# Moving w1's transposes between the gate and the up product, and starting the remaining pages of wo at head 2 of the backward part

## The chip, the cores and the metric

The kernel runs on one core of one Trainium2 chip. The metric is the device time of one execution in microseconds (us). Executions of one kernel spread by about 0.2%, with now and then one that is 0.5% longer, so I compare medians and ratios with 95% intervals, and I read the mechanism in the trace of one profiled execution. The engines are called PE (matrix), DVE (vector), ACT (scalar), POOL (GpSimd) and SP (sync). One megabyte of V, or of an output, is one transfer of one head.

## The reference, cut to what matters

It is one decode step of a transformer layer and its whole gradient: attention over cached K and V of 4 batches x 32 heads x 4096 positions x 128, then a gated feed-forward layer with w1, w3 and w2.

```python
h  = x + attention(layernorm(x), k_cache, v_cache, wq, wo)     # 4 x 1 x 512
h2 = h + (silu(hh @ w1) * (hh @ w3)) @ w2                      # hh = layernorm(h)
# outputs: h2, and by jax.vjp the gradients of x, k_cache, v_cache, wq, wo, w1, w3, w2
```

The gradients of the two caches are 128 heads x 1 MB each. They are outer products: for each head, gv = P (x) dO and gk = dS (x) q. V has to be read twice, once for the forward product and once, transposed, for dP = V dO.

## The kernel before: the parts that the change touches

SBUF has 23 slots of 1 MB. K, V, weights and outputs all take their place in them. Slots are handed out in the order in which they came free, so an output may have to wait until an older output has left its slot.

The middle part lies between forward and backward. It makes the gate and the up product, transposes w1 and w3 in place, and makes dn, from which the first gradients follow:

```python
tunits = deque((nm, i, k) for nm in ("w3", "w1") for i in range(2) for k in range(0, FC, 4))
...
for wi, wt in enumerate((w1, w3)):                 # gate product, then up product (L816 after)
    for fc in range(FC):
        for cc in range(DC):
            nc.tensor.matmul(gu_ps[:, wi, fc, :], lhsT=w13_view(wt, cc)[:, fc * P:(fc + 1) * P], ...)
...                                                # silu and its derivative, on DVE
w13T(len(tunits), "ssssvsvssvvsvsvv")              # 112 transposes; "s"/"v": copied back by ACT/DVE
for jj in range(DC):
    for (lt, wt) in ((d_upT_bf, w3), (d_gateT_bf, w1)):
        ...                                        # dn, 112 products
while len(free) > 2:
    load_V2()
```

For dP a head needs its column of dO, and for gv it needs its row of dO. Both come from wo, in four pages of eight heads (eight of the model's 32, so 32 of the 128 that are counted as head 0, 1, 2 and so on below). Page 0 is done in the middle part. The others are done piece by piece by a generator that is stepped once per head. For each page it has four wo units (eight transposes and one copy) and then one step that makes the columns and rows of dO:

```python
def dO_columns(h0, h1, ps, tag):
    ...                                                    # PE: 32 products into dOT_ps
    nc.vector.tensor_copy(out=dOT_bf[:, s0:s1], in_=dOT_ps[:, s0:s1])              # L735
    nc.vector.tensor_tensor(out=dOT_f[:, s0:s1], in0=dOT_bf..., in1=OT_f..., op=ALU.mult)  # L736
def dO_rows(h0, h1, ps_, tag_):
    nc.tensor.transpose(pq[0:s1, :], dOT_bf[:, 0:s1], ident_b[:])                  # L741
    ...
    nc.tensor.matmul(c_ps[:, s0:s1], lhsT=ones_f[:], rhs=dOT_f[:, s0:s1], ...)     # L744
    nc.vector.tensor_copy(out=c_rep[:, s0:s1], in_=c_ps[:, s0:s1])                 # L745

def rest_of_dO():
    for pg in range(1, H // 8):
        while wo_units and wo_units[0] < 4 * (pg + 1):
            woT_unit(psT, wo_units.popleft(), "s")
            yield
        dO_columns(8 * pg, 8 * pg + 8, psg, "gps")
        dO_rows(8 * pg, 8 * pg + 8, psg, "gps")
        mid_w["wo"][pg].give()                             # the page's slot comes free here
        yield
```

The backward part:

```python
S0 = 15
...
front(0)
step("o")                       # one step of rest_of_dO
for s in range(NH):
    prefetch()
    if s + 1 < NH:
        ...
        front(s + 1)            # PE, ACT: every 4th head replicate rows; 32 transposes of V; dP
        grad_V(s + 1)           # DVE: gv (2.29 us), then its 1 MB output
    grad_K(s)                   # DVE: dS, gk (2.29 us), then its 1 MB output
    if s < S0:
        step("o")
    else:
        step("s", ...)          # side work: gradients of the weights
```

## Time and profile before

| before | |
|---|---|
| time | 1732.32 us (1732.11 to 1735.81, 3 runs); with a fourth run, 1735.24, the median is 1733.78 |
| profiled execution | 1741.45 us, span of the core 1739.7 us |
| moved by DMA | 707.86 MB, at 419 GB/s in a good stretch |
| underfed stretch at the turn from forward to backward | 702 to 748 us, 12.6 us lost |
| first gv given to DMA | 712.7 us |
| dO of page 1 | at head 3, 743 to 745 us |

To read the profile, "lost" is the time that a stretch would have saved at 419 GB/s: its length times (1 - GB/s / 419). Lost isn't the same as idle. In the windows that the prediction shows, the column before GB/s is the share of time in which the DMA engines were busy; it is about 1.01 in a full window.

### The profile page before, as it was taken

The numbers are of one execution on the slowest core, as the hardware profiler recorded it, in microseconds if no ns is written. First come the engines' busy times: TensorE is split into PE (matmuls) and PEld (weight loads), VectorE is DVE, ScalarE is ACT, GpSimd is POOL, SyncE is SP. The second block draws the span as 40 slices with busy tenths as digits, with TensorE's granted clock in tenths as the row PEclk, the third lists the DMA queues.
The fourth block names the chain that finished last, engine by engine and source line by source line (L and its number), as shares of the span: only waits on it lengthen the run. The fifth ranks groups of instructions, "written<-read, shape, count | busy, mean of one in ns | idle before, by whom it ended". The sixth has DMA issues, their size and how long they took to land.

```text
span 1739.7 us, 44047 instructions
## 1 busy us (share of the span) xinstructions
PE 1331.1 (77%) x19014; PEld 1123.0 (65%) x19014; DVE 1253.8 (72%) x1388; ACT 958.4 (55%) x1469; POOL 445.6 (26%) x808
## 2 busy tenths in 40 slices
PE   5888888888888888877888887856685878778662
PEld 4667666676666666766777777755563556556562
DVE  5989899889998996567567667665583555665673
ACT  3455445444444454666555564546674667667552
POOL 1211232222222221223123222222231232223331
PEclk8999999999999999676555565558665655555555
DMA  9999999999999999899999999999999999999997
GB/s 398 410 419 418 419 418 419 419 416 418 411 419 408 418 404 392 317 397 418 416 415 421 419 412 414 413 417 419 423 411 368 420 416 406 412 405 410 411 418 290
DMA packets 107179, 707.86 MB, mean 407 GB/s; under 512 B 11284, under 2 KB 18976, under 8 KB 24040
## 3 DMA queue, kind: packets, MB, share of 16 engines
q1 hardware_dynamic: 66880, 422.60, 59.3%
q0 software_dynamic: 39712, 282.37, 39.8%
q8 instruction: 149, 2.44, 0.5%
q14 instruction: 46, 0.38, 0.1%
q10 hardware_dynamic: 392, 0.07, 0.0%
HBM read 422.59 MB, written 282.34 MB: 405 GB/s over the span
## 4 chain that ended last, share of the span: by engine, by line
DMA 42%; DVE 6%; PE 6%; ACT 5%; issue 4%; POOL 0%; SPq 0%; POOLq 0%; DVEq 0%; ACTq 0%
DMA out_dram<-gk 27%; DMA out_dram<-gv 6%; ACT VT L760 4%; DMA wq<-in_A_wq_dram 3%; DVE gk L1114 2%; PE pt_tps L759 2%; DVE gv L1114 2%; DMA out_dram<-gw 2%; DMA out_dram<-gwo 2%; DMA w<-in_B_w_dram 1%; DMA wo<-in_A_wo_dram 1%; PE gps L907 1%; PE dP_ps L1108 0%; DVE PK L418 0%; PE pt_w L562 0%
## 5 line engine op out<-in xcount | busy, mean ns | idle before, releaser
L760 ACT COPY VT<-pt_tps 128x1024 bf16<-128x1024 bf16 x512 | 492.7, 1015 | 244.6 <-PE pt_tps L759 131.3
L759 PE MATMUL pt_tps<-ident_b,V 128*128 128x128 bf16 x4096 | 456.8, 294 | 118.9 <-ACT VT L760 97.7
L759 PEld LDWEIGHTS <-V 128*128 128x128 bf16 x4096 | 405.5, 139 | 184.6 <-issue 154.9
L1114 DVE TENSOR_TENSOR gv<-P,reps 128x4096 bf16<-128x4096 bf16 x128 | 293.5, 2293 | 258.3 <-DMA out_dram<-gk 98.0
L1114 DVE TENSOR_TENSOR gk<-dS,reps 128x4096 bf16<-128x4096 bf16 x128 | 293.4, 2292 | 81.8 <-DMA out_dram<-gv 48.2
L433 PE MATMUL M_ps<-PK,Vn 128*128 128x130 bf16 x4096 | 285.6, 222 | 51.0 <-DMA Vn<-in_A_v_cache_dram 50.4
L418 DVE TENSOR_TENSOR PK<-Kn,PK 128x4096 bf16<-128x4096 bf16 x128 | 292.3, 2284 | 33.5 <-POOL PK L414 33.2
L433 PEld LDWEIGHTS <-Vn 128*128 128x128 bf16 x4096 | 252.4, 99 | 72.6 <-DMA Vn<-in_A_v_cache_dram 66.9
L325 DVE STREAM_TRANSPOSE KT<-Kn 128x512 f32<-128x512 f32 (+1 forms) x321 | 250.7, 797 | 0.3 <-issue 0.2
L320 ACT COPY KT<-pt_tps 128x1024 bf16<-128x1024 bf16 x128 | 129.5, 1012 | 191.0 <-PE pt_tps L319 149.5
L1108 PE MATMUL dP_ps<-dOT_bf,VT 128*128 128x1 bf16 x4096 | 152.6, 166 | 67.8 <-ACT VT L760 64.5
L1108 PEld LDWEIGHTS <-VT 128*128 128x128 bf16 x4096 | 141.1, 104 | 80.3 <-ACT VT L760 76.8
L1139 POOL DMA_DIRECT2D out_dram<-gk x128 | 68.4, 534 | 360.9 <-DVE gk L1114 225.2
L1125 POOL DMA_DIRECT2D out_dram<-gv x128 | 68.7, 537 | 325.2 <-DVE dSt L1132 258.1
L331 POOL TENSOR_TENSOR W<-qrep,wmask 128x128 bf16<-128x128 bf16 x128 | 124.1, 969 | 81.6 <-PE S_ps L351 67.0
L414 POOL COPY PK<-P_all 128x64 bf16<-128x64 bf16 x128 | 32.6, 254 | 422.3 <-ACT P_all L408 419.3
L1098 POOL COPY P<-P_all 128x64 bf16<-128x64 bf16 x128 | 126.3, 988 | 0.0
L408 ACT COPY P_all<-pt_P 32x64 bf16<-32x64 bf16 x256 | 52.1, 204 | 60.6 <-PE pt_P L404 58.4
L319 PE MATMUL pt_tps<-ident_b,Kn 128*128 128x128 bf16 x1024 | 80.4, 223 | 0.0
L443 PE MATMUL kP_ps<-PK,onesw 128*32 128x512 bf16 x1024 | 79.2, 386 | 0.0
L319 PEld LDWEIGHTS <-Kn 128*128 128x128 bf16 x1024 | 61.9, 99 | 25.6 <-issue 25.6
L397 ACT ACTIVATE Pn<-E,rl 128x1024 bf16<-128x1024 f32 x64 | 73.7, 1152 | 3.2 <-DVE rl L394 3.2
(228 smaller groups left out, 1292.3 us busy)
## 6 DMA issues: line engine op xcount, KB each, us to landing
Kn<-in_A_k_cache_dram SPq DMA_DIRECT2D x128, 1024.0 KB, 15.7
Vn<-in_A_v_cache_dram SPq DMA_DIRECT2D x128, 1024.0 KB, 15.8
V<-in_A_v_cache_dram SPq DMA_DIRECT2D x128, 1024.0 KB, 10.9
out_dram<-gv POOLq DMA_DIRECT2D x128, 1024.0 KB, 24.6
out_dram<-gk POOLq DMA_DIRECT2D x128, 1024.0 KB, 24.6
wq<-in_A_wq_dram SPq DMA_DIRECT2D x8, 1024.0 KB, 14.0
out_dram<-gw POOLq DMA_DIRECT2D x6, 896.0 KB, 28.8
wo<-in_A_wo_dram SPq DMA_DIRECT2D x4, 1024.0 KB, 13.2
```

The lines of the kernel that those rows point to most:

```text
L319: nc.tensor.transpose(pt[:, i, :], Kn[:, c * GW + i, :], ident_b[:])
L320: nc.scalar.copy(out=KT[:, c * GW:(c + 1) * GW, :], in_=pt[:])
L325: nc.vector.transpose(out=KT[:, c * w_:(c + n) * w_], in_=Kn[:, c * w_:(c + n) * w_])
L331: nc.gpsimd.tensor_tensor(out=W[:, hl], in0=qrep[:, :, s:s + 1].to_broadcast([P, 4, 32]), in1=wmask[:, hl, None, :].to_broadcast([P, 4, 32 ...
L418: nc.vector.tensor_tensor(out=PK[:, :, 0:Dh].rearrange("p j (r t) -> p j r t", t=2), in0=Ks[s].heads().rearrange("p j (r t) -> p j r t", t=2),
L433: nc.tensor.matmul(hold["M"][:], lhsT=Vn[:, j, :], rhs=PK[:, j, :], start=(j == 0), stop=(j == SJ - 1))
L443: nc.tensor.matmul(hold["kP"][32 * q:32 * (q + 1), :, :], lhsT=ones_window(w), rhs=PK[:, j0:j0 + 4, 0:Dh], start=(w == 0 and c == 0), stop ...
L759: nc.tensor.transpose(pt[:, i, :], Vn[:, g * GW + i, :], ident_b[:])
L760: nc.scalar.copy(out=VT[:, g * GW:(g + 1) * GW, :], in_=pt[:])
L1098: nc.gpsimd.tensor_copy(out=P2s[s][:], in_=P_all[:, s, :, None].to_broadcast([P, SJ, 2]))
L1108: nc.tensor.matmul(dP_ps[:, j:j + 1], lhsT=VT[:, j, :], rhs=dOT_bf[:, s:s + 1], start=True, stop=True)
L1114: nc.vector.tensor_tensor(out=dst.rearrange("p j (r t) -> p j r t", t=2), in0=col2[:, :, None, :].to_broadcast([P, SJ, Dh // 2, 2]), in1=r ...
```

## The change

It has two parts. **Part (a)**: 28 transposes of the first half of w1 go between the gate and the up product, where PE was waiting for the second half of w3, and dn takes w1 first. **Part (b)**: the generator for wo is first stepped at head 2, not ahead of head 0, so no wo unit stands in the way of the first heads. The dO step of page 1 thereby moves from head 3 to head 6, and the side work starts at head 18, not 15.

```diff
-    tunits = deque((nm, i, k) for nm in ("w3", "w1") for i in range(2) for k in range(0, FC, 4))
+    tunits = deque((nm, i, k) for nm in ("w1", "w3") for i in range(2) for k in range(0, FC, 4))
@@ in the loop of the gate and up products
+            if wi == 0:
+                w13T(4, "sv")
@@
-        w13T(len(tunits), "ssssvsvssvvsvsvv")
+        w13T(len(tunits), "sssvsvsvsvvs")
@@
-            for (lt, wt) in ((d_upT_bf, w3), (d_gateT_bf, w1)):
+            for (lt, wt) in ((d_gateT_bf, w1), (d_upT_bf, w3)):
@@
-        S0 = 15
+        O0, S0 = 2, 18
@@
         front(0)
-        step("o")
         for s in range(NH):
@@
             grad_K(s)
-            if s < S0:
+            if s >= S0:
+                step("s", 1 if s < S0 + 44 else 3)
+            elif s >= O0:
                 step("o")
-            else:
-                step("s", 1 if s < S0 + 44 else 3)
```

## The prediction

> **What bounds the kernel now.** I read the page first, for how evenly the DMA engines are fed over the span, then the windows where they are not, then the chain of waits and the timeline inside those windows.
>
> ```profile
> DMA  9999999999999999899999999999999999999997
> GB/s 398 410 419 418 419 418 419 419 416 418 411 419 408 418 404 392 317 397 418 416 415 421 419 412 414 413 417 419 423 411 368 420 416 406 412 405 410 411 418 290
> ...
> HBM read 422.59 MB, written 282.34 MB: 405 GB/s over the span
> ```
>
> Each number is one fortieth of the span, 43.5 us. A good slice moves 419 GB/s. 707.86 MB at 419 GB/s take 1689 us of the 1740 us span, so the kernel is bound by bytes, and only time in which the DMA engines are underfed can be won. Two slices in the interior fall well short: the 17th (317), where the forward part turns into the backward part, and the 31st (368). The last one is the end of the span: the last 1 MB outputs land there 2.45 us apart, so the queue is full to the end, and a microsecond of DMA time won earlier should come out at the end whole. The changed lines run in the 17th slice and its neighbours. Its windows (columns: window, length, busy time of PE, PEld, DVE, ACT, POOL, then granted clock, DMA share, GB/s):
>
> ```profile
> 702.00:710.00 8.00, 7.08 (x183) 6.82 (x180) 2.48 (x11) 2.92 (x4) 0.57 (x3) 0.80 0.76 284
> 710.00:714.00 4.00, 2.84 (x23) 2.22 (x21) 2.80 (x4) 2.18 (x3) 0.99 (x3) 0.50 0.08 35
> 716.00:728.00 12.00, 10.16 (x136) 9.22 (x134) 9.87 (x9) 9.61 (x10) 6.50 (x9) 0.50 0.80 326
> 728.00:734.00 6.00, 5.41 (x69) 4.94 (x66) 2.77 (x3) 4.59 (x5) 1.09 (x3) 0.50 0.95 291
> 734.00:742.00 8.00, 6.25 (x75) 5.38 (x76) 4.72 (x4) 5.43 (x8) 0.53 (x1) 0.57 1.00 421
> 742.00:748.00 6.00, 4.86 (x75) 4.38 (x76) 3.35 (x7) 2.95 (x4) 3.06 (x4) 0.70 0.96 291
> ```
>
> Lost against 419 GB/s, length times (1 - GB/s / 419): 2.6, 3.7, 2.7, 1.8, 0 and 1.8 us, together 12.6 us. This is the ceiling of any gain here: 0.7% of the time. Two causes. Until the first gradient tile gv exists, all slots hold V and nothing can be written (702 to 714). Then heads come every 6.6 us with two 1 MB outputs each and no V load yet due (716 to 734): 2.1 MB in 6.6 us is 319 GB/s. What paces both, from the timeline and the chain:
>
> ```profile
> 687.81 1.59 PE L816 MATMUL gu_ps<-hhatT,w 128*128 128x4 bf16 x58 [0.68 <-DVE hhatT L809]
> ...
> 691.21 1.60 PE L816 MATMUL gu_ps<-hhatT,w 128*128 128x4 bf16 x54 [1.81 <-DMA w<-in_B_w_dram]
> ```
>
> ```profile
> 700.31 1.72 PE pt_w L562 x28
> 702.03 2.81 PE dn_ps L845 x112
> ...
> 721.55 0.89 PE pt_wo L571 x8
> 722.46 1.02 ACT wo L215
> 723.52 1.03 PE pt_tps L759 x8
> 724.57 1.02 ACT VT L760
> 725.63 1.03 PE pt_tps L759 x8
> 726.68 1.02 ACT VT L760
> 727.75 0.37 PE dP_ps L1108 x8
> 728.13 0.89 PE pt_wo L571 x8
> ```
>
> In the middle PE idles 1.8 us for the second half of w3, then does all 112 transposes of w1 and w3 (692.9 to 702.0) ahead of the product dn. In the first heads PE and ACT take turns: one unit of wo (8 transposes, one copy), four units of V, the product dP. From one wo unit to the next is 6.58 us. Heads 4 and 5, at 737.7 and 745.0, have no wo unit between their first transpose and the end of dP and take 5.5 and 5.4 us. So one wo unit costs about 1.15 us in this stretch.
>
> **What the Trainium skill says.** "DMA: Bandwidth & Descriptors", section Specifications, gives 435 GB/s as the fabric's ceiling and about 358 GB/s as a core's HBM share. The trace holds 419, above the second, so the measured 419 is my full rate. The same page, section "Anatomy of one DMA", fits a DMA as about 2.0 us plus bytes / 436e3, which is 4.4 us for 1 MB. The first writes, alone on the engines, landed 3.6 to 4.7 us after issue; with V loads beside them 8 to 10 us. "TensorE: Matmul & The Clock Gate", section "What's actually happening", has a free-running activity window of 3.4 us that puts the PE at half or full clock. The trace steps at 689.75 (half), 696.58 (full), 706.82 (half): 36 transposes at half clock took 3.82 us (106 ns each), 28 at full clock 1.72 us (61 ns each). So where the clock steps fall is a lottery in the middle part. The 4-column products of L816 took the same 28 to 30 ns each in both.
>
> **The change, part by part.** No work is removed or added: the built program has the same number of instructions on PE and DVE. They move.
>
> (a) 28 transposes and four copies of the first half of w1 go between the gate and the up product. The gate product ends near 689.4, and four PSUM buffers are there, so no copy holds them up. Five transposes run before the clock drops, 23 at 106 ns: until about 692.2. The up product then starts about 1.0 us later than now (691.2) and ends near 693.8. 84 transposes are left. At the old clock steps 22 of them run until 696.6, the other 62 at 61 ns until 700.4. Walking through the copies (ACT 1.01 us, DVE 0.69 us, four buffers, in the new order) I get 700.7, because ACT has three in a row first. dn then starts at 700.7 and not 702.0: **1.3 us won**, 0 to 2 with the clock. dn takes w1 before w3, as it must, and the chain behind it is unchanged, so the first gv moves from 710.1 to about 708.8.
>
> (b) The generator of wo units is first stepped at head 2. Ahead of the first units of head 4 (the replicated rows that gv of head 4 waits for) four wo units stand now, and one afterwards. DVE shows what that costs now: it waits 6.15 us at 737.2 for those rows. 3 x 1.17 = 3.5 us go. The dO columns of page 1 also leave head 3 (at 743 they cost DVE a 1.8 us wait and delay gv of head 5 to 745.35) and come at head 6. Walking on head by head with 4 to 5 us per landing without V loads and 9 to 10 with them, gk of head 3 starts at 735.0 (now 740.0), gk of head 5 at 748.8 (now 754.2), gv of head 8 at 761.5 (now 765.3), gk of head 7 at 763.9 (now 769.9). The lead is about 5 us, (a) included.
>
> (c) Given back: pages 1 to 3 of wo hold their slots three heads longer, and side work starts three heads later. With five slots rotating, a head needs about (landing + 5.1) / 2 us, from the reuse order (gv takes the slot of the gk three heads before). With a landing of 10 us that is 7.6 us for 3.1 MB, 414 GB/s. That is nearly the full rate, so I charge 0.3 us. The side work has some 200 steps and should end near head 114 instead of 111, still 13 heads before the end: no cost. The wo units now fall where DMA is the bound: hidden.
>
> Sum: 1.3 + 3.8 - 0.3 = 4.8 us of 1732.3, so **1727.5 us**.
>
> **Rivals.** First, slots become the bound: without page 1's slot, heads 4 to 7 stop on landings (gv of head 6 already waited 1.00 us for a gk). The windows after 748, at 419 with one slot more, do not speak for it; it would take back 2 to 3 us: 1730. Second, the clock stays at half through all of the transposes, because the work is moved into what used to be the idle window: 84 at 106 ns end near 703, a microsecond later than now, which leaves about 1730. Third, the gain is lost later: at 1336 to 1340 DMA is again underfed (160 GB/s), because V loads stood up to 36 us behind queued writes and the loads of w2. Shifting side work by three heads re-deals this stretch, for plus or minus 2 to 3 us; the bytes-bound tail does not repair it. Fourth, the lead grows: if heads 1 to 3 run faster and V loads also start 3 to 4 us earlier, up to 8 of the 12.6 us come back: 1724.
>
> **Range and chances.** These rivals spread some 3 to 5 us about the estimate, and runs of the kernel before spread 3.7 us: 1722.5 to 1732.5. Faster by over 2% would need 35 us, nearly three times what is lost here; slower by over 2% needs a new stall as long. Both 1%.
>
> **What would show it.** In the changed profile: no PE idle before the up product; dn starting about 1.3 us earlier; first gv near 709; replicated rows of head 4 near 732 and not 736.5; 716 to 734 above 370 GB/s; the whole stretch 702 to 748 losing 7 to 8 us and not 12.6; a 17th slice near 350. I am wrong if DVE waits for landings of gk in heads 4 to 7 make up for it, or if the stretch at 1310 to 1350 loses much more or less than now.

## More of the kernel before

The profiled execution is 5.6 us longer than the longest of the four others, so its span isn't the kernel's usual one.

The prediction shows the page, the windows and the chain. One more view of before is wanted for the comparison: the waits of DVE from 715 to 770 us. Its columns are the waiting instruction, what it waited for, us in total, times, and the longest.

```profile
DVE gv L1114 <- ACT reps L1089: 6.1, 1, 6.1
...
DVE dOT_bf L735 <- PE dOT_ps L733: 1.8, 1, 1.8
```

The first line is the wait for the replicated rows of head 4, behind the wo units. The other is the dO step of page 1, where DVE waits for PE. The waits for outputs to leave their slots, left out here, are 6.7 us in all.

## The result, and the profile after

A ratio here compares the fast runs of two kernels from the same rounds, so it isn't quite the ratio of the medians.

| | median us | lowest to highest | runs |
|---|---|---|---|
| before | 1733.78 | 1732.11 to 1735.81 | 4 |
| after | 1731.46 | 1730.04 to 1733.69 | 4 |

The ratio is 0.9987, with a 95% interval of 0.997 to 1.0005. The point of 1727.5 us was 4.0 us too low, and the range held the time. I had predicted a gain of 4.8 us, and 2.3 us came.

The line of the page of after that answers to that of before:

```profile
GB/s 399 410 418 418 419 418 419 418 418 417 415 417 408 418 402 391 342 392 424 418 416 412 413 411 414 414 413 418 422 423 421 425 419 411 412 413 411 407 417 294
```

The 17th slice went from 317 to 342 GB/s, and the 31st, once 368, is full. Don't read the spans of the two profiles (1739.7 and 1729.8 us) as the gain: the profiled execution of before was an unusually long one. More on that below.

The windows of after (window, length, busy time of PE, PEld, DVE, ACT, POOL, granted clock, DMA share, GB/s):

```profile
702.00:710.00 8.00, 5.96 (x101) 5.71 (x97) 3.90 (x11) 4.44 (x5) 0.57 (x3) 0.79 0.72 282
710.00:714.00 4.00, 3.91 (x55) 3.41 (x55) 2.96 (x5) 1.75 (x4) 3.60 (x5) 0.52 0.64 264
716.00:728.00 12.00, 10.04 (x155) 9.34 (x154) 10.87 (x9) 8.84 (x10) 5.71 (x7) 0.50 0.90 302
728.00:734.00 6.00, 4.70 (x46) 3.98 (x47) 0.21 (x1) 3.72 (x5) 0.38 (x2) 0.50 1.00 421
734.00:742.00 8.00, 7.08 (x107) 6.52 (x105) 5.63 (x5) 6.29 (x8) 1.31 (x3) 0.57 1.01 418
742.00:748.00 6.00, 2.67 (x48) 2.22 (x45) 4.10 (x4) 3.60 (x5) 1.31 (x3) 0.97 1.02 423
760.00:780.00 20.00, 13.45 (x171) 11.85 (x172) 16.55 (x19) 11.80 (x14) 7.05 (x11) 0.63 0.95 363
```

And the one window of before that the prediction had no reason to show:

```profile
760.00:780.00 20.00, 12.97 (x224) 11.60 (x223) 12.21 (x10) 12.83 (x15) 2.63 (x6) 0.79 1.01 420
```

Three things are to be seen. From 710 to 714 DMA moved 264 GB/s and not 35: the first gradients came earlier. From 728 to 748 it is full, where before had two windows at 291. From 760 to 780 it is at 363 where before had 420: a hole that wasn't there. In numbers, from 700 to 750 us before lost 12.5 us and after 7.9 us, which is 4.6 us better. From 760 to 780 before lost nothing and after 2.7 us.

The first thing is part (a). The timeline of PE in the middle of after (start, duration, line, output<-inputs, shapes, count, idle before and who ended it):

```profile
687.46 1.54 PE L816 MATMUL gu_ps<-hhatT,w 128*128 128x4 bf16 x56 [0.67 <-DVE hhatT L809]
688.86 2.47 PE L562 MATMUL pt_w<-ident_b,w 128*128 128x128 bf16 x28
691.12 1.68 PE L816 MATMUL gu_ps<-hhatT,w 128*128 128x4 bf16 x56
...
692.73 6.92 PE L562 MATMUL pt_w<-ident_b,w 128*128 128x128 bf16 x84
699.48 0.49 PE L847 MATMUL dn_ps<-d_gateT_bf,w 128*128 128x4 bf16 x14
```

The 28 transposes fill the old wait of 1.81 us, and the up product starts at 691.12 us, as early as before (691.21). dn starts 2.4 us earlier (in the chains, 699.64 against 702.03 us).

The second thing is part (b). The waits of DVE in after, from 715 to 770 us:

```profile
DVE gv L1116 <- DMA out_dram<-gk: 15.6, 5, 6.5
```

The wait for the replicated rows of head 4 is gone. In its place DVE waits for outputs to leave their slots, 15.6 us in five waits for a gk and 1.0 us in one for a gv. These waits don't cost what they look like: during most of them DMA is full (418 to 423 GB/s from 728 to 748), so the core is at its bound.

The third thing is the hole. First PE, then DVE, in after's timeline around the dO step of page 1:

```profile
757.85 0.99 PE L733 MATMUL dOT_ps<-dhT,wo 128*128 128x4 bf16 x32
763.25 0.31 PE L741 MATMUL pdo_rows<-ident_b,dOT_bf 128*64 128x128 bf16 x1 [4.40 <-DVE dOT_bf L735]
```

```profile
758.00 2.29 DVE L1116 TENSOR_TENSOR gv<-P,reps 128x4096 bf16<-128x4096 bf16 x1 [2.24 <-DMA out_dram<-gk]
...
760.80 2.29 DVE L1116 TENSOR_TENSOR gk<-dS,reps 128x4096 bf16<-128x4096 bf16 x1
763.01 0.18 DVE L735 CAST dOT_bf<-dOT_ps 128x32 bf16<-128x32 f32 x1
```

PE has the columns of dO ready at 758.84 us and needs a cast of 0.18 us for its next instruction. DVE has that cast behind a gv, which waited for a landing until 758.00, and a gk. PE stands idle for 4.40 us, and behind it stand the transposes of the next head, from which the next outputs come. Some 5 us later the hole begins: 317 GB/s from 768 to 772 and 242 from 772 to 776 us, with a DMA share of 0.89 in both. So the queue runs thin, but that is less than half of it. Over the whole window from 760 to 780 the share is 0.95, which is about 1.2 us of idle DMA out of 2.7 us lost. The rest is again a slow V load (771.8 to 776.5 us, 506 ns a packet). The Trainium skill, "PSUM — Partial Sum Buffer", section "Engine vs sequencer instructions", says that the queues of ScalarE, VectorE and GpSimdE are strictly first in, first out, and that PE's matrix products stay in program order. The trace agrees: nothing overtakes the cast for 4.40 us.

In before the same step stood at head 3, and there DVE waited 1.8 us for PE. The window around it, 742 to 748, lost 1.8 us, but mostly by slow packets, so what the step cost there isn't shown.

### The profile page after: what moved, and what is told of

It is laid out like the page before. It is cut to its first block, busy times and chain, and to the rows that moved or that the text cites. A ratio compares the mean times of both kernels' runs of the same rounds, so it can differ in the third digit from the quotient of the medians.

```text
span 1729.8 us, 44048 instructions
## 1 busy us (share of the span) xinstructions
PE 1328.0 (77%) x19014; PEld 1121.1 (65%) x19014; DVE 1253.1 (72%) x1388; ACT 959.0 (55%) x1469; POOL 432.5 (25%) x808
## 4 chain that ended last, share of the span: by engine, by line
DMA 38%; PE 8%; ACT 7%; DVE 6%; issue 3%; ACTq 0%; POOL 0%; DVEq 0%; POOLq 0%
DMA out_dram<-gk 22%; DMA out_dram<-gv 9%; ACT VT L760 5%; DMA wq<-in_A_wq_dram 3%; DVE gk L1116 3%; PE pt_tps L759 3%; DVE gv L1116 2%; DMA out_dram<-gwq 2%; DMA out_dram<-gw 1%; PE gps L909 1%; PE M_ps L433 1%; DVE PK L418 1%; PE dP_ps L1110 1%; PE pt_w L562 0%; PE rep_ps L1088 0%
## 5 line engine op out<-in xcount | busy, mean ns | idle before, releaser
L1100 POOL COPY P<-P_all 128x64 bf16<-128x64 bf16 x128 | 112.0, 876 | 0.0
## 6 DMA issues: line engine op xcount, KB each, us to landing
Kn<-in_A_k_cache_dram SPq DMA_DIRECT2D x128, 1024.0 KB, 15.6
```

The source lines that it names most:

```text
L1100: nc.gpsimd.tensor_copy(out=P2s[s][:], in_=P_all[:, s, :, None].to_broadcast([P, SJ, 2]))
```

## The experiments

My theory after reading the result was this: part (a) gains some 2 us and passes them to the end. Part (b) removes the loss at heads 1 to 4 and at 742 to 748, and gives it back in the hole at 760 to 780, which the dO step makes because PE and DVE wait for each other there. Rivals: the hole comes from the lack of a slot (page 1 of wo is held three heads longer); it comes from the replicated rows of head 8, which follow that step; or (b) is simply worth nothing, and the hole is chance.

Twelve runs were made in four jobs, each job on one chip and with its own timings of before. First the times. "400 MB at" is when the profiled execution had moved 400 MB, a measure of the lead that isn't blurred by the spread of whole runs.

| run | edit | median us (before of that job) | ratio, 95% | first gv at | 400 MB at |
|---|---|---|---|---|---|
| profile of before | | | | 712.7 | 978.1 |
| profile of after | (a)+(b) | 1731.46 (1733.78) | 0.9987 (0.997 to 1.0005) | 710.4 | 976.3 |
| c_before | none: before again | 1735.0 (1732.8) | 1.0014 (0.9998 to 1.0029) | 711.9 | 978.5 |
| c_mid_only | (a) alone | 1730.63 (1732.8) | 0.9991 (0.9978 to 1.0004) | 710.1 | 975.2 |
| c_wo_only | (b) alone | 1734.11 (1732.8) | 1.0008 (0.9993 to 1.0022) | 712.5 | 977.7 |
| c_after | (a)+(b) again | 1731.56 (1732.8) | 0.9998 (0.9984 to 1.0012) | 709.9 | 975.7 |
| d_cast_act | casts of the dO step off DVE | 1730.46 (1734.62) | 0.9979 (0.9964 to 0.9993) | 710.6 | 976.9 |
| d_o_early | dO step ahead of gv and gk | 1731.49 (1734.62) | 0.999 (0.9968 to 1.0012) | 709.8 | 974.6 |
| d_nv5 | one slot fewer for V | 1732.96 (1734.62) | 0.9995 (0.998 to 1.0011) | 710.1 | 974.6 |
| d_o1 | wo from head 1 | 1732.28 (1734.62) | 0.9983 (0.9968 to 0.9998) | 712.0 | 978.2 |
| e_delay | 112 idle transposes added | 1736.85 (1733.48) | 1.0025 (1.0011 to 1.0039) | 716.6 | 981.8 |
| e_o8 | wo from head 8 | 1729.84 (1733.48) | 0.9982 (0.997 to 0.9994) | 710.4 | 975.9 |
| e_mid_nv5 | (a) alone, one slot fewer for V | 1732.9 (1733.48) | 0.9998 (0.9986 to 1.001) | 711.1 | 980.0 |
| f_split | rows of dO one head after the columns | 1731.22 (1734.56) | 0.9975 (0.9951 to 1.0) | 710.6 | 973.6 |

And the loss against 419 GB/s, in us, by stretch (where 760 to 780 lost over 1 us, DMA was busy for 0.95 to 0.99 of it, so idle DMA is about half of the loss or less in each):

| stretch | before | c_before | c_wo_only | c_mid_only | after | c_after | d_cast_act | d_o_early | d_nv5 | d_o1 | e_delay | e_o8 | e_mid_nv5 | f_split |
|---|---|---|---|---|---|---|---|---|---|---|---|---|---|---|
| 700 to 750 | 12.5 | 10.8 | 10.0 | 8.3 | 7.9 | 6.9 | 7.8 | 6.9 | 8.2 | 10.4 | 13.5 | 7.7 | 13.0 | 7.6 |
| 760 to 780 | 0.0 | 0.0 | 2.2 | 0.0 | 2.7 | 1.6 | 2.9 | 1.9 | 0.4 | 2.0 | 2.1 | 0.7 | 0.0 | 0.1 |

**c_before: the kernel before against itself.** It tells how small a difference the times can show.

> The kernel before, unchanged, timed against itself. All theories: ratio 1.000 with an interval of about 0.001 to each side, which is what this way of timing can tell apart. Its profile is a second sample of the kernel before: the loss in 702 to 748 us against 419 GB/s should repeat as 12 to 13 us if it belongs to the program. The second underfed stretch (1310 to 1350, 6 us lost in the first profile) should repeat if it belongs to the program, and be gone or elsewhere if it was chance of that one execution.

The same program came out at 1.0014, with an interval that just reaches 1. So times alone settle no difference below about 0.15%, which is 2.6 us, all that is at stake here. The losses by stretch repeat to within about 2 us over 50 us (12.5 and 10.8).

**c_mid_only: part (a) alone.** Its edit is the change without the lines of part (b), from `S0 = 15` on.

> Only part (a): w1 transposed between gate and up, wo units as in the kernel before. Theory 1 (the middle part wins, all of it reaches the end): the first gv is issued about 2.0 to 2.3 us earlier than before, the loss in 702 to 748 falls by about 2 us, ratio 0.9988. Rival (the win is swallowed by the first heads, which are paced by PE and ACT, or by later waits): ratio 1.000.

The first gv came at 710.1 us, 1.8 us before c_before's, and 400 MB had been moved 3.3 us earlier. There is no hole from 760 to 780. The median lies 2.2 us below that of before, with an interval that still holds 1.

**c_wo_only: part (b) alone.** Its edit is only those lines.

> Only part (b): wo units from head 2, middle part as before. Theory 1 (the win of the first heads, 2.5 to 3.5 us by the end of head 5, is given back by about 2.4 us where page 1's dO columns now stand at head 6): loss in 702 to 750 down by 2 to 3 us, a new loss of 2 to 3 us in the 25 us after the dO columns of page 1, ratio 0.9995 to 1.000. Rival (the win of (b) is kept): ratio 0.998.

Two windows of it, and below them the one of c_before that answers to the first:

```profile
742.00:760.00 18.00, 14.28 (x216) 13.18 (x215) 10.39 (x9) 12.02 (x13) 2.61 (x6) 0.50 1.01 424
760.00:780.00 20.00, 12.57 (x171) 11.18 (x168) 17.45 (x18) 10.24 (x13) 7.00 (x11) 0.59 0.98 372
```

```profile
742.00:760.00 18.00, 14.64 (x225) 13.20 (x221) 13.10 (x14) 12.99 (x15) 6.98 (x9) 0.72 1.00 369
```

The hole moved: 369 GB/s became 424 in the first window, and the second is at 372. With shares of 1.00 and 0.98, what was lost in either is mostly slow packets. Its PE line at the dO step is that of after:

```profile
764.80 0.31 PE L741 MATMUL pdo_rows<-ident_b,dOT_bf 128*64 128x128 bf16 x1 [4.51 <-DVE dOT_bf L735]
```

From 716 to 780 us c_wo_only lost 6.0 us, the two profiles of before 6.7 and 5.7. So (b) alone is worth 0.7 to -0.3 us there, and the time doesn't contradict it (1.0008, 0.9993 to 1.0022). On top of (a) it is no better: 400 MB had been moved at 975.2 us in c_mid_only, and at 976.3 and 975.7 with both parts. The hole is not chance: the hole is in every profile of a kernel that has part (b) with its dO step near head 6, unless something was done about it.

**c_after: the changed kernel again.**

> The changed kernel again. Theory 1: ratio 0.9985 to 0.999, and its second profile shows the same new underfed stretch (760 to 780, about 2.4 us lost, with an idle PE of over 4 us ahead of the dO rows of page 1). Rival (that stretch was chance): the stretch is full this time and the ratio is nearer to 0.997.

The hole repeats (1.6 us), with PE idle for 3.12 us ahead of the rows of dO. The ratio was 0.9998 here and 0.9987 in the first comparison.

**d_cast_act: the two casts and the copy of the dO step on ACT and POOL instead of DVE** (pages 1 to 3 only).

```diff
-        nc.vector.tensor_copy(out=dOT_bf[:, s0:s1], in_=dOT_ps[:, s0:s1])
-        nc.vector.tensor_tensor(out=dOT_f[:, s0:s1], in0=dOT_bf[:, s0:s1], in1=OT_f[:, s0:s1], op=ALU.mult)
+        (nc.scalar.copy if h0 else nc.vector.tensor_copy)(out=dOT_bf[:, s0:s1], in_=dOT_ps[:, s0:s1])
+        (nc.gpsimd if h0 else nc.vector).tensor_tensor(out=dOT_f[:, s0:s1], in0=dOT_bf[:, s0:s1], in1=OT_f[:, s0:s1], op=ALU.mult)
@@ and in dO_rows
-        nc.vector.tensor_copy(out=c_rep[:, s0:s1], in_=c_ps[:, s0:s1])
+        (nc.scalar.copy if h0 else nc.vector.tensor_copy)(out=c_rep[:, s0:s1], in_=c_ps[:, s0:s1])
```

> The changed kernel, but for pages 1 to 3 the two small evacuations of the dO columns (dOT_bf and c_rep) are made by ACT and the product dOT_f by POOL, so that none of them stands behind gv and gk in DVE's order. Theory 1 (DVE, held at gv of head 7 by the landing of an older gk, reaches the small cast late; PE, in order, waits for it, and V loads and the next heads start late): PE's idle time before the dO rows of page 1 falls from 3.1 to 4.4 us to under 1 us, the loss in 760 to 780 from 1.6 to 2.7 us to under 0.7 us, 400 MB are moved by about 974 us (changed kernel: 975.7 and 976.3), ratio about 0.9985. Rival (five slots alone underfeed the DMA there, whatever PE does): the idle goes but the loss of about 2 us stays, ratio as the changed kernel, 0.999.

The experiment missed its aim. A line of PE's timeline, then two of POOL's:

```profile
763.82 0.64 PE L744 MATMUL c_ps<-dOT_f,ones_f 128*128 128x32 f32 x2 [5.16 <-POOL dOT_f L736]
```

```profile
762.96 0.53 POOL L1141 DMA_DIRECT2D out_dram<-gk  x1 [2.27 <-DVE gk L1116]
763.51 0.26 POOL L736 TENSOR_TENSOR dOT_f<-dOT_bf,OT_f 128x32 f32<-128x32 bf16 x1
```

With the cast on ACT, PE waited only 0.28 us for it, but the product on POOL stands behind the issue of a gk that DVE hadn't made yet, and PE waited 5.16 us for that. The wait only changed its engine, and the hole stayed at 2.9 us. Its time, 0.9979, can't be put down to a hole that didn't shrink.

**d_o_early: the dO step ahead of gv and gk in the program's order.**

```diff
                 front(s + 1)
+                if O0 <= s < S0:
+                    step("o")
                 grad_V(s + 1)
             grad_K(s)
             if s >= S0:
                 step("s", 1 if s < S0 + 44 else 3)
-            elif s >= O0:
-                step("o")
```

> The changed kernel, but the step of the wo generator stands between the front of head s+1 and gv of head s+1, so that the cast of the dO columns comes ahead of the gv that waits for a slot in DVE's order. Theory 1: as for the cast on ACT, PE idle before the dO rows of page 1 under 1 us, loss in 760 to 780 under 0.7 us, ratio about 0.9985. Rival: the loss of about 2 us stays.

PE's idle time is gone (0.28 us), but DVE now waits 3.44 us for PE's columns of dO before it may begin gv. The hole is 1.9 us. In both orders that were tried, one of the two engines waits for the other.

**d_nv5: one slot fewer for V, so one more for outputs.** The edit is `NV2 = 6` to `NV2 = 5`.

> The changed kernel with a ring of 5 V tiles in place of 6, so one slot more rotates among VT, gv and gk from head 3 on. Theory 1: DVE's waits for landings of gk at gv of heads 4 to 7 (6.5, 2.3, 4.4 and 2.2 us in the first profile) shrink to under half, with them the PE idle before the dO rows of page 1 (under 1.5 us), and the loss in 760 to 780 is under 0.7 us. Later a ring of 5 leaves less lead for V loads, so more may be lost after 1000 us: ratio 0.998 to 1.002. Rival (the hole in 760 to 780 has nothing to do with slots): it stays at about 2 us.

The hole shrank to 0.4 us, though PE still idled 3.65 us at the dO step. But another opened earlier:

```profile
734.00:742.00 8.00, 6.08 (x111) 5.47 (x109) 7.88 (x7) 6.22 (x7) 4.49 (x5) 0.79 0.99 332
```

That is 1.7 us lost where after lost nothing, at a DMA share of 0.99, so again slow packets (a V load from 736.8 to 742.0 us, 490 ns each). The times show no gain. So slots seem to have a share in it: with a sixth rotating slot the same idle time of PE hardly shows as a hole, which suggests that it takes both, a PE held up and too few outputs in flight to bridge it. As V loads moved too in this run, that isn't a clean proof.

**d_o1: wo from head 1.** The edit is `O0, S0 = 2, 18` to `1, 17`. The dO step then falls one head earlier and no longer stands right ahead of the replicated rows of head 8.

> The changed kernel with the wo generator begun at head 1 instead of 2 (side work at 17), so the dO columns of page 1 stand at head 5, not just ahead of the replicated rows of head 8. Theory 1: gv of head 6 also waits over 4 us for a landing in the changed kernel, so PE idles 2 us or more ahead of these dO rows and some 1 to 2 us are lost in the 20 us after it, now about 750 to 765. Rival (the loss comes from the dO rows meeting the replicated rows of head 8): loss under 0.5 us there and in 760 to 780. Ratio 0.999 in the first case, 0.998 in the second.

The hole stayed (2.0 us), and PE idled 3.84 us, so the neighbourhood of those rows is not the cause. This profile also showed the clock lottery: PE went to half clock already at 687.9 us and stayed there for 10.2 us, and the first gv came at 712.0 us. Of that, 0.9 us are a later gate product (688.33 us). From its start to dn it took 12.8 us, against 14.1 in before and 12.0 in after.

**e_delay: the middle part made longer on purpose.** 112 transposes without a reader, right after the real ones.

```diff
+        for k in range(14):
+            pt_d = psT.tile([P, 2, 4, P], BF16, tag="tps", name="pt_dummy")
+            for i in range(8):
+                nc.tensor.transpose(pt_d[:, i // 4, i % 4, :], w13_view(w3, i % 4)[:, k * P:(k + 1) * P], ident_b[:])
```

> The changed kernel with 112 more transposes of w3 into PSUM tiles that nobody reads, ahead of the product dn: the middle part is lengthened by what PE needs for them, 112 at 61 to 106 ns or 7 to 12 us. Theory (the middle part stands alone in front of the writes; its time passes to the end whole): the first gv is issued d = 7 to 12 us later than in the changed kernel, the moment when 400 MB are moved comes d later to within 1.5 us, and the time is d longer: ratio 1.004 to 1.007. Rival (the later stages take part of it back, as the small gain in the timing of part (a) could suggest): 400 MB under 0.7 d later and a ratio under 1.003.

Its first gv was given to DMA at 716.62 us, 6.2 us later than in after and 6.7 later than in c_after. I had expected 7 to 12 us and a ratio of 1.004 to 1.007; both came out smaller. 400 MB came 5.5 to 6.1 us later, the span of the profile was 5.0 to 6.2 us longer, and the ratio to before of 1.0025 lies 0.0027 to 0.0038 above the two of the changed kernel, which is 4.7 to 6.6 us. So a microsecond of the middle part is worth about a microsecond at the end, within these spreads, and the 2 us that (a) wins there are no local matter.

**e_o8: wo from head 8.** The edit is `O0, S0 = 8, 24`. If the dO step makes the hole, the hole goes with it to head 12.

> The changed kernel with the wo generator begun at head 8 (side work at 24), so that page 1's dO columns stand at head 12, near 800 us. Theory 2 (this step costs the DMA about 2 us wherever it stands, as long as five slots rotate and it breaks the even flow of outputs and V loads): 760 to 780 is full (loss under 0.7 us) and 1.5 to 3 us are lost in the 25 us after that step, so that 400 MB are moved no earlier than in the changed kernel (975.5 to 976.5 us). Rival (the hole is a chance of that moment; with heads 0 to 7 free of wo work the gain of the first heads is kept): no loss over 0.7 us after the step, and 400 MB moved by 973.5 to 974.5 us. Ratio 0.999 or 0.998.

```profile
760.00:780.00 20.00, 14.53 (x199) 13.43 (x197) 12.49 (x11) 12.57 (x13) 3.92 (x9) 0.50 1.01 405
804.00:824.00 20.00, 12.48 (x169) 10.98 (x170) 15.87 (x16) 11.12 (x14) 5.43 (x10) 0.67 1.00 388
```

It went: 0.7 us are lost in the old place, and 388 GB/s from 804 to 824 us are 1.5 us in the new one, with PE idle for 4.53 us. It was the fastest median of all (1729.84), but 400 MB came no earlier (975.9), and its interval (0.997 to 0.9994) overlaps that of most others, so I don't claim it as better.

**e_mid_nv5: part (a) alone with one slot fewer for V.** An attempt at something better than both kernels.

> An attempt at a better version: only part (a), with a ring of 5 V tiles, so one slot more for outputs. If slots limit heads 1 to 5, the loss in 716 to 750 falls from 3.9 us (part (a) alone) to under 3 us, 400 MB are moved by 974 us and the ratio is about 0.998; if the late first V loads matter more (as the 1.7 us lost at 734 to 742 in the changed kernel with 5 V tiles may show), the loss is as large or larger and the ratio 0.999 to 1.000.

It failed. From 734 to 742 us it lost 3.3 us, at a DMA share of 0.70, so here mostly for want of transfers, and 400 MB came at 980.0 us.

**f_split: the rows of dO one head after the columns.** If the hole comes from PE and DVE waiting for each other within one step, it should go when a whole head lies between the two halves.

```diff
                 dO_columns(8 * pg, 8 * pg + 8, psg, "gps")
-                dO_rows(8 * pg, 8 * pg + 8, psg, "gps")
                 mid_w["wo"][pg].give()
                 yield
+                dO_rows(8 * pg, 8 * pg + 8, psg, "gps")
+                yield
@@
-        O0, S0 = 2, 18
+        O0, S0 = 2, 21
```

> The changed kernel, but the rows part of the dO step (transpose, ones product) is made one head later than its columns part, so that neither PE waits for DVE's cast nor DVE for PE at head 6 (side work from head 21). Theory 1 (the wait of the in-order engines for each other at this step makes the hole): no PE idle over 1.5 us before the dO rows, loss in 760 to 780 under 0.7 us and under 1 us in 780 to 850, 400 MB moved by about 974 us, ratio about 0.998. Rival (with five slots the hole comes anyway, because gv of head 8 waits for the landing of the gk three heads before and V loads come in a bunch after it): 1.5 to 2.5 us are still lost between 755 and 790, and 400 MB are moved at 975.5 to 976.5.

```profile
757.27 0.99 PE L733 MATMUL dOT_ps<-dhT,wo 128*128 128x4 bf16 x32
...
765.50 0.31 PE L741 MATMUL pdo_rows<-ident_b,dOT_bf 128*64 128x128 bf16 x1
```

```profile
760.00:780.00 20.00, 16.57 (x223) 15.08 (x223) 15.45 (x17) 14.63 (x17) 5.68 (x11) 0.61 1.01 417
```

The second PE line shown has no idle time ahead of it, and the window is full. DVE's waits for landings of gk were 16.8 us from 715 to 770 us, more than in after, and they cost nothing. 400 MB were moved at 973.6 us, 2.1 to 2.7 us ahead of the two profiles of the changed kernel, which is the size of the hole. So the hole is shown to need the mutual wait: it went with the step to head 12, and it was gone, slow load and all, when the wait was taken out.

The wait alone isn't enough. In before the dO step of page 2 held PE up too, and DMA stayed full:

```profile
780.19 0.34 PE L741 MATMUL pdo_rows<-ident_b,dOT_bf 128*96 128x128 bf16 x1 [2.88 <-DVE dOT_bf L735]
```

```profile
780.00:800.00 20.00, 16.80 (x188) 15.11 (x189) 14.68 (x16) 13.73 (x16) 7.60 (x10) 0.50 1.01 419
```

PE stood idle for 2.8 to 3.7 us at a step of page 2 or 3 in c_before, c_mid_only, d_o1, e_delay, e_mid_nv5 and f_split as well, and none of them lost over 0.2 us in the 20 us after it. By then the slot of page 1 is back, so one slot more rotates, as in d_nv5. That the hole takes both, a wait and only the five slots of the first heads, fits these profiles, but no run varied the slots alone.

The lead of f_split wasn't kept: by 600 MB f_split was at 1455.2 us and after at 1455.4. From 1000 to 1300 us it lost 2.8 us against 1.7 and 1.2 in the two profiles of the changed kernel, and from 1300 to 1500 1.9 against 0.5 and 1.3. Whether splitting the step causes this later loss or chance does stays open. The time (1731.22) is not told apart from that of the changed kernel. Its ratio of 0.9975 owes something to a before with three runs above 1741 us in that job.

## Why the prediction was right or wrong

The time lay in the range, but that says little: before's 1732.3 us lies in it too, so no gain at all would have fitted. The gain was half of the one predicted, and its two terms were both off: (a) was too small, and (b), the larger one, was as good as zero. That as much as half came is in part luck, since (a) made good some of what (b) lacked.

**What bounds the kernel: right.** e_delay shows that time lost in the middle part comes out at the end at about one to one.

**Part (a), "1.3 us won": the right mechanism, too small.** The first gv went from 712.7 to 710.4 us, of which 0.35 us are an earlier gate product (687.46 against 687.81) that isn't due to the change. That leaves about 2.0 us. From the start of the gate product to dn it took 14.1 us in before and 14.0 in c_wo_only, and 12.0 in after and in four more profiles whose half-clock spell was as long (6.8 us). The spell is a matter of luck: with (a) it was 3.4 us in four profiles (11.4 to 11.5 us to dn) and 10.2 in d_o1 (12.8), and in c_before, where it began ahead of the gate product, the old order took only 12.3. The term that was mis-sized is "The up product then starts about 1.0 us later than now". It started at 691.12 us, not later at all: the gate product ended 0.4 us earlier than I took it (nearly all of that is its earlier start), and the 28 transposes took 2.33 us in the chain, 83 ns each and not nearly all at 106. After the up product, before took 9.2 us for 112 transposes up to dn and after 6.7 us for 84, so 28 transposes left the path for 2.5 us. The rival that the clock would spoil it is seen in one profile, d_o1, and only in part.

**Part (b), "3 x 1.17 = 3.5 us go": this is where the prediction failed, twice.** First, PE did reach the rows of head 4 early, at 729.1 us and not 735.5, as predicted. But gv of head 4 didn't start until 733.79:

```profile
733.79 2.29 DVE L1116 TENSOR_TENSOR gv<-P,reps 128x4096 bf16<-128x4096 bf16 x1 [6.47 <-DMA out_dram<-gk]
```

It waited for a gk that was issued at 722.34 us and landed at 733.67, after 11.3 us. "Walking on head by head with 4 to 5 us per landing without V loads" would have had it land by 728. The first V load came in between, at 723.8 to 728.6 us, and went slowly: its 8 KB packets took 515 ns on average where 309 is usual. The predicted "716 to 734 above 370 GB/s" came out at 342 (302 up to 728, then 421). The walk's own marks show how the 5 us of lead melted: gk of head 3 began at 736.5 us (735.0 predicted, 740.0 in before), gk of head 5 at 753.5 (748.8; 754.2), gv of head 8 at 765.4 (761.5; 765.3). Secondly, "The wo units now fall where DMA is the bound: hidden" and "so I charge 0.3 us". For the wo units that holds, but not for the dO step at their end. I had written down that this step makes DVE wait 1.8 us at head 3, and treated its move to head 6 as pure gain. It made PE wait 4.40 us there, and the hole of 1.6 to 2.7 us came with it. c_wo_only shows the net of (b): 0.7 to -0.3 us, for 3.5 predicted. The sum of the two parts is then 2 us.

**Slips in its working.** The sum puts 3.8 us for (b), where the working has 3.5. At 106 ns, 26 transposes and not 22 fit before 696.6. And it took all of 716 to 734 for heads with "no V load yet due", while in before a V load was issued at 726.68 us and was moving in 728 to 734: there it took slow packets for an underfed DMA. The total for 702 to 748, "losing 7 to 8 us", held (7.4 us in the same windows), though the loss was shared out otherwise than it said.

**The rivals.** The first (slots) was half right: the waits for landings came as it said, but they mostly lay beside a full DMA, and f_split removed the hole with as many of them left. The fourth (the lead grows) had its condition met and still failed: the first V load after the turn was issued at 721.5 us, 5.2 us earlier than in before, but it was the slow one. The third, that the stretch at 1310 to 1350 would be dealt anew, is what the profiles show and what stays open. The three profiles of kernels without (a) lost 6.3 to 7.3 us from 1300 to 1500 us (404 to 406 GB/s at a DMA share of 1.00, so much of it is slow packets). Ten of the eleven with (a) lost under 2 us, d_o_early 4.7. But before's unprofiled runs (1732.11 to 1735.81 us) are not longer than after's by that much, and its profiled ones are the long ones (1741.45; c_before 1740.32 against 1731.56 to 1735.9 without the profile), though three of the eleven timings of before beside f_split were as long. It isn't a matter of an early start alone either, since e_delay starts later than before and lost 0.6 us there. I leave it out of the gain and can't explain it.

**How sure the 2 us are.** No comparison of the change or of (a) alone shows them: the intervals of after, c_mid_only and c_after all hold 1. Those of d_cast_act, d_o1 and e_o8 don't, but these kernels differ in more than (a). Together they do better. All ten comparisons of kernels that have (a) without the added delay had a ratio below 1, from 0.9975 to 0.9998, and their mean is 0.9988, which is 2.1 us. The two without it were at 1.0008 and 1.0014. As those kernels differ in other ways and share their timings of before within a job, this is an argument and not a measurement.

## What to carry to other kernels

When an engine waits for a transfer ahead of a serial stretch, work that is needed later and whose data are there already is worth its whole duration as far as it fits into the wait. A step in which two in-order engines hand results to each other (PE, DVE, PE, DVE) is a meeting point: moving it moved the stall here, and what removed it was a head's worth of other work between its halves. In a kernel bound by bytes, read a wait together with the GB/s of its window: in f_split 16.8 us of waiting beside a full DMA cost nothing there, and in after 4.4 us of an idle PE were followed by a loss of 2.7. And read GB/s together with the DMA share: a window at 291 GB/s with a share of 0.95 isn't underfed but slow, and feeding it earlier needn't help.

## What the Trainium skill lacked or had wrong

- "DMA: Bandwidth & Descriptors", section "Anatomy of one DMA — SWDGE (gpsimd) path", has a fit for a DMA by itself (4.4 us for 1 MB by estimate from it; the first gv took 4.21 us here). The page gives no time for a write that shares the engines with a read: the gk issued at 722.34 us took 11.3 us, while one 1 MB V load passed with packets of 515 ns for the usual 309. No page and no run shows why this load is slow. It is also seen at 771.8 to 776.5 us (506 ns), in the hole, and at 743.6 to 748.7 us in before (484 ns), and in f_split only at the first load (416 ns).
- "TensorE: Matmul & The Clock Gate", section "Part 4: PE-mode transpose", says that the full clock doesn't engage for transposes. Here the clock went to full at 696.58 us in before, when PE had done nothing but transposes for 3.7 us, and 28 of them then took 1.72 us (61 ns each), against 106 ns each at half clock. The section's figure of about 275 ns is for one transpose, and single ones fit it (216 to 314 ns in before's profile), but it has no figure for a row of them.
- "PSUM — Partial Sum Buffer", section "Engine vs sequencer instructions", has the in-order queues, but no page draws what follows for two engines that hand results back and forth: PE idle for 4.40 us for a cast of 0.18 us, and for 5.16 us when the product was given to POOL, whose queue stood behind an output that wasn't made yet.
